# The first two batches of a retention and mixer kernel in another order on every engine, casts moved between engines, and w1 in four tiles

## The chip, the core and the metric

The kernel runs on one core of a Trainium2 chip. The metric is the device time of one execution in microseconds; the time given for a kernel is the median of its runs. The core has five engines that work side by side: TensorE (PE, with its weight loads shown as PEld), VectorE (DVE), ScalarE (ACT), GpSimd (POOL) and SyncE (SP, which here only issues transfers). Each engine takes its instructions strictly in the order in which they are written, and waits where one of them waits.

## The reference, cut

```python
def _attn_ref(q, k, v):                      # q, k, v: [8, 8, 576, 64]
    scores = (1.0 / np.sqrt(64)) * np.matmul(q, k.transpose(0, 1, 3, 2))
    gamma = 1.0 - 2.0 ** (-5.0 - np.arange(8))
    rel = pos[:, None] - pos[None, :]
    Dmat = np.where(rel >= 0, gamma[:, None, None] ** rel[None], 0.0)
    return np.matmul(scores * Dmat[None], v)

def _moe_ref(x, U, V, w_ch1, w_ch2):         # x: [8, 576, 512]
    xt = x.transpose(0, 2, 1)
    h = xt @ U @ V                           # U: [576, 32], V: [32, 576]
    u = x + h.transpose(0, 2, 1)
    ch = np.maximum(u @ w_ch1, 0.0) @ w_ch2  # [512, 2048], [2048, 512]
    return u + ch
```

The first function's heads, laid side by side, are the x of the second. Inputs and output are float32; the kernel computes in bfloat16 with float32 sums.

## The kernel before, in words

The decay of the retention is split into a factor for each query row (`qscale`) and one for each row of V (`vscale`, with the scale of the scores in it). What is left is a causal mask of ones, so a running sum of k times scaled v can be carried from chunk to chunk.

Two batches make a pair: 1,152 rows, nine chunks of 128 rows. Chunk 4, called J, holds the last 64 rows of the first batch (LO) and the first 64 of the second (HI). Later pairs go chunk by chunk through `section`, with their q and k transposed by DMA. The first pair goes by four *units* of 256 rows (0 and 1 in the first batch, 2 and 3 in the second), plus J's halves, and PE transposes it. A unit's q, k and v come as two half tiles each, of four heads (`load_u` on SP's queue). The pool `stage` holds 15 such tiles.

The steps of a unit u are these. `cast_u(u, j, hh, engine)` casts half hh of q (j = 0) or k (j = 1) to bfloat16, and `scale_u` multiplies v by `vscaleU`. `T_u(u, j, engine)` transposes on PE and copies out on the engine named; the copy of q also reorders. `SC_u` makes scores, `mask_u` masks them on DVE (line 674). `ST_u` adds k times v to the sum `acc` in PSUM, and `Sblk` copies its two diagonal blocks to SBUF as state. `RV_u` and `QS_u` add masked scores times v and q times state in the PSUM tile `po`; `XS_u` multiplies by `qscale` on DVE into x (line 712). J has the same steps with `_J`, and `XS_J` is at line 796.

Then comes the mixer of the first batch. `to_xT` transposes x in PSUM with an identity (lines 899 to 905). `MA` multiplies x by U into `a_sb` (line 437). Four matmuls with `V4` (lines 921 to 926) add h in the same PSUM tiles, and four copies on ACT and DVE make `uT` (lines 928 to 934). `make_uo` makes a copy of U shifted by half a chunk for the second batch. `Y1` is the first channel product: for each of 16 blocks f of 128 columns of w1, four matmuls of 512 columns (line 525), then a Relu on ACT (line 530). Y1 tiles rotate over the three PSUM tiles of `ps_big`. `Y2` is the second product (line 559).

w1 is one tile of 2048 columns, cast to bfloat16 on its way. `load_w1(fb)` brings a quarter of it, the columns of blocks 4 fb to 4 fb + 3, and is issued on POOL's queue, as are the pairs of w2 blocks (`load_w2`; `gated_w2` first reads a Y1 result).

The order is written out by hand under `manual_schedule`: `early_consts`, then `startup` (units 0 and 1, J's LO, the first mixer), then `first_stretch` (Y1 blocks of the first batch with units 2 and 3, J's HI and the second mixer between them). `warm(n)` issues n matmuls on the identity whose results nobody reads. From then on `merge` lays the steps of later chunks over the blocks of Y1 and Y2 by shares of their cost. `prep(g)` casts q and k of chunk g, scales v and issues the transpose on SP; its `load` comes earlier. The order list counts the first pair's chunks, so batch 2 begins with chunk NI = 9. For the second batch `merge` starts after six Y1 blocks of its own (`y1_left`); `prep(11)` stands at 0.06 of that stretch.

Of the kernel before, what the change touches and what calls it, by code (L numbers as in the profile page):

```python
# [36 lines left out]
def kernel(  # L37
# [17 lines left out]
    P = 128  # L55
# [59 lines left out]
    w1_sb = consts.tile([P, NCC, dff], BF16, name="w1_sb")  # L115
# [79 lines left out]
    W1B = 512  # L195

    def load_w1(fb):
        nc.gpsimd.dma_start(
            out=w1_sb[:, :, fb * W1B:(fb + 1) * W1B],
            in_=moe_w_ch1[:, fb * W1B:(fb + 1) * W1B].rearrange("(c p) f -> p c f", p=P),  # L200
        )
# [308 lines left out]
    def y1_items(par, by_seg=False):  # L510
# [6 lines left out]
        def Y1(f, seg):  # L517
# [6 lines left out]
            for cc in range(NCC):  # L524
                nc.tensor.matmul(  # L525
                    ps[:, 0:n, :], w1_sb[:, cc, f * P:(f + 1) * P],
                    st["uT", par][:, c0:c0 + n, cc, :],
                    start=(cc == 0), stop=(cc == NCC - 1),
                )
# [67 lines left out]
    def load_u(u, which):  # L597
        b = u // 2
        t0 = 2 * P * (u % 2) + HALF * b
        for j in which:  # L600
            dram = (q, k, v)[j]
            for hh in range(2):
                t = stage.tile([P, H, D], FP32, tag="stage", name="stage_t")
                un[u]["f", j, hh] = t
                nc.sync.dma_start(  # L605
                    out=t.rearrange("p (h j) d -> p h (j d)", j=2),
                    in_=dram[b, 4 * hh:4 * hh + 4, t0:t0 + 2 * P, :].rearrange(
                        "h (p j) d -> p h (j d)", j=2),
                )

# [23 lines left out]
    def T_u(u, j, eng):  # L634
        pst = ps_big.tile([P, 2 * NHP, P], BF16, tag="big", name="pst")
        for jj in range(2):
            for hp in range(NHP):
                nc.tensor.transpose(  # L638
                    pst[:, jj * NHP + hp, :], un[u][j][:, jj, hp * P:(hp + 1) * P], ident)
        t = qkT_pool.tile([P, 2 * NHP, P], BF16, tag="qkT", name="qkT")  # L640
# [7 lines left out]
        if eng is nc.scalar:  # L648
            nc.scalar.activation(out=o, in_=i_, func=AF.Copy)  # L649
        else:  # L650
            eng.tensor_copy(out=o, in_=i_)
# [162 lines left out]
    def pss_tile():  # L814
        return ps_s.tile([P, NHP, P], FP32, tag="pss", name="pss")

    def cast_unit(u):
        for j in (1, 0):
            for hh in range(2):
                cast_u(u, j, hh, nc.gpsimd)  # L820

    def startup():
        load_u(0, (1, 0))
        load_v_rows()
        load_u(1, (1, 0))
        load_u(0, (2,))
        load_u(1, (2,))
        load(0, J, (1, 0, 2), seg=0)
        load_u_rows()
        load(0, J, (1, 0, 2), seg=1)  # L830
        load_u(2, (1, 0, 2))
        load_u(3, (1, 0, 2))
        nc.gpsimd.memset(x_of(0, J)[HI, :], 0.0)

        warm(10)
        cast_unit(0)
        T_u(0, 1, nc.vector)
        warm(5)
        nc.scalar.activation(out=V_b, in_=V_f, func=AF.Copy)
        T_u(0, 0, nc.scalar)  # L840
        make_v()
        warm(3)
        SC_u(0, 0, ps_sc, "psc")
        mask_u(0, 0)
        cast_unit(1)
        T_u(1, 1, nc.scalar)
        SC_u(0, 1, ps_o, "po")
        mask_u(0, 1)
        warm(2)
        T_u(1, 0, nc.scalar)  # L850
        scale_u(0, 0, nc.gpsimd)
        load_w1(0)
        scale_u(1, 0, nc.gpsimd)
        scale_u(1, 1, nc.gpsimd)
        cast_qk(0, J, LO, nc.gpsimd, js=(0,))
        scale_v(0, J, LO, nc.gpsimd)
        load_w1(1)
        cast_qk(0, J, HI, nc.gpsimd)
        scale_v(0, J, HI, nc.gpsimd)
        load_w1(2)  # L860
        scale_u(0, 1, nc.vector)
        warm(6)
        SC_u(1, 0, ps_sc, "psc")
        mask_u(1, 0)
        SC_u(1, 1, ps_o, "po")
        mask_u(1, 1)

        accA = pss_tile()
        accB = ps_big.tile([P, NHP, P], FP32, tag="big", name="pss2")
        ST_u(0, LO, accA, True)  # L870
        Sblk(accA, 0)
        ST_u(0, ALL, accB, True)
        Sblk(accB, 1)
        cast_qk(0, J, LO, nc.scalar, js=(1,))
        po_u(0, ps_sc, "psc")
        warm(2, ps_big, "big")
        RV_u(0, 0)
        RV_u(0, 1)
        QS_u(0, 1, 0)
        XS_u(0)  # L880
        warm(1, ps_big, "big")
        ST_u(1, LO, accB, False)
        Sblk(accB, 2)
        warm(1, ps_big, "big")
        RV_u(1, 0)
        RV_u(1, 1)
        T_J(LO, nc.vector)
        ST_u(1, HI, accB, False)
        Sblk(accB, 3)
        SC_J(LO)  # L890
        mask_J(LO)
        QS_u(1, 0, 1)
        QS_u(1, 1, 2)
        XS_u(1)
        make_ue()

        xT = [ps_big.tile([P, dm], FP32, tag="big", name="xT") for _ in range(3)]

        def to_xT(i, ccs):
            for cc in ccs:  # L900
                nc.tensor.matmul(
                    xT[cc][:, i * P:(i + 1) * P],
                    x_of(0, i)[:, cc * P:(cc + 1) * P], ident,
                    start=(i == 0), stop=True, skip_group_check=True,
                )

        for i in range(2):
            to_xT(i, range(3))
        RV_J(LO)
        QS_J(3)  # L910
        XS_J(LO)
        warm(2, ps_sc, "psc")
        xT.append(ps_sc.tile([P, dm], FP32, tag="psc", name="xT"))
        for i in range(2, J):
            to_xT(i, range(3))
        for i in range(J):
            to_xT(i, (3,))
        MA, _, _, _ = mixer_items(0, 0, split=True)
        MA((ps_o, "po"))
        warm(1)  # L920
        for cc in range(NCC):
            g = slice(cc * R, (cc + 1) * R)
            nc.tensor.matmul(
                xT[cc], st["a", 0][g, :], V4[g, HALF:HALF + 4 * P],
                start=False, stop=True, skip_group_check=True,
            )
        warm(1)
        for cc in range(NCC):
            o = st["uT", 0][:, :, cc, :]
            i_ = xT[cc].rearrange("p (s t) -> p s t", t=P)  # L930
            if cc % 2 == 0:
                nc.scalar.activation(out=o, in_=i_, func=AF.Copy)
            else:
                nc.vector.tensor_copy(out=o, in_=i_)
# [7 lines left out]
    def first_stretch():  # L942

        ys = iter([fn for _, fn in y1_items(0)])

        def y(n):
            for _ in range(n):
                fn = next(ys, None)
                if fn is not None:
                    fn()  # L950

        _, MH0, _, outs0 = mixer_items(0, 0, split=True)
        MA1, MH1, MT1, outs1 = mixer_items(0, 1, split=True)
        y(1)
        make_uo()
        y(3)
        T_J(HI, nc.scalar, ps_s, "pss")
        y(1)
        SC_J(HI)
        mask_J(HI)  # L960
        y(1)
        acc = pss_tile()
        ST_J(HI, acc)
        Sblk(acc, 0)

        def unit(u, slots, last):
            if last:
                load_w1(u)
            for hh in range(2):
                cast_u(u, 1, hh, nc.gpsimd)  # L970
            cast_u(u, 0, 0, nc.gpsimd)
            cast_u(u, 0, 1, nc.gpsimd)
            if last:
                load(*order[NI], (1, 0, 2), gate=True)
                load(*order[NI + 1], (1, 0, 2))
            scale_u(u, 0, nc.gpsimd)
            scale_u(u, 1, nc.gpsimd)
            if not last:
                y(1)
            T_u(u, 1, nc.vector)  # L980
            T_u(u, 0, nc.scalar)
            y(2)
            SC_u(u, 0, ps_sc, "psc")
            mask_u(u, 0)
            y(1)
            ST_u(u, LO, acc, False)
            Sblk(acc, slots[1])
            SC_u(u, 1, ps_sc, "psc")
            mask_u(u, 1)
            if not last:  # L990
                RV_u(u, 0)
                ST_u(u, HI, acc, False)
                Sblk(acc, slots[2])
            else:
                y(1)
                load(*order[NI + 2], (1, 0, 2))
                RV_u(u, 0)
            QS_u(u, 0, slots[0])
            QS_u(u, 1, slots[1])
            RV_u(u, 1)  # L1000
            XS_u(u)
            if last:
                RV_J(HI)
                XS_J(HI)

        unit(2, (0, 1, 2), False)
        unit(3, (2, 3), True)
        load_w2(0)
        load_w2(2)
        load_w2(4)  # L1010
        xT = [None] * NCC

        def to_xT(ccs, chunks):
            for cc in ccs:
                if xT[cc] is None:
# [42 lines left out]
        for f in range(6):  # L1058
            Y1(f, 1)
# [103 lines left out]
```

## Time and profile before

| what | value |
|---|---|
| median of three runs | 319.55 us (318.63 to 320.24) |
| profiled execution | 318.86 us, of which the traced span is 317.1 us |
| PE busy in the span | 306.5 us (97%) |
| DVE, ACT, POOL busy | 165.0, 137.6, 90.8 us |
| granted TensorE clock | 1.00 |
| read from HBM, written to it | 36.85 MB, 9.44 MB |
| first Y1 matmul | 24.36 us from the span's start |
| w1 issues on POOL | 13.30, 19.48, 24.54, 34.94 us |
| w2 issues on POOL, first three | 40.48, 41.24, 41.95 us |

A row of the timeline has the start in microseconds, the duration, the engine, the line, the operation, the tiles it writes and reads, their shapes, and in brackets the idle time of the engine before it and what ended that. The profile is one execution, so its sums are held against its own 318.86 us. Busy time counts `warm` too, and a matmul counts from its issue to its modelled end.

### The profile page before, as it was taken

The numbers are of one execution on the slowest core, as the hardware profiler recorded it, in microseconds if no ns is written. First come the engines' busy times: TensorE is split into PE (matmuls) and PEld (weight loads), VectorE is DVE, ScalarE is ACT, GpSimd is POOL, SyncE is SP. The second block draws the span as 40 slices with busy tenths as digits, with TensorE's granted clock in tenths as the row PEclk, the third lists the DMA queues.
The fourth block names the chain that finished last, engine by engine and source line by source line (L and its number), as shares of the span: only waits on it lengthen the run. The fifth ranks groups of instructions, "written<-read, shape, count | busy, mean of one in ns | idle before, by whom it ended". The sixth has DMA issues, their size and how long they took to land.

```text
span 317.1 us, 9092 instructions
## 1 busy us (share of the span) xinstructions
PE 306.5 (97%) x3903; PEld 168.4 (53%) x3929; DVE 165.0 (52%) x320; ACT 137.6 (43%) x282; POOL 90.8 (29%) x138
## 2 busy tenths in 40 slices
PE   7999899999999999999999999999999999999996
PEld 2564554554544544467744545467654444467544
DVE  5562466535998753892358723992258714200012
ACT  2747657770122474137820474237820453057300
POOL 5765833523241523243221320343211100100000
PEclk9999999999999999999999999999999999999999
DMA  7999999999999999999959899899925104110022
GB/s 211 246 194 258 251 202 205 194 237 209 203 241 190 280 206 199 186 244 190 220 96 215 199 173 193 162 210 245 201 68 138 68 2 83 68 66 1 2 87 79
DMA packets 151320, 53.30 MB, mean 168 GB/s; under 512 B 131984, under 2 KB 148752, under 8 KB 151280
## 3 DMA queue, kind: packets, MB, share of 16 engines
q1 hardware_dynamic: 144512, 40.40, 69.8%
q0 software_dynamic: 6768, 12.32, 16.3%
q8 instruction: 30, 0.49, 0.7%
q14 instruction: 10, 0.08, 0.1%
HBM read 36.85 MB, written 9.44 MB: 146 GB/s over the span
## 4 chain that ended last, share of the span: by engine, by line
PE 83%; DMA 5%; SPq 5%; DVE 3%; issue 2%; ACT 1%; POOL 0%; DVEq 0%; ACTq 0%
PE ps_y L525 37%; PE ps_y L559 36%; DMA w_sb<-in_moe_w_ch_dram 3%; SPq L605 3%; DMA stage_t<-in_v_dram 2%; PE po L377 1%; SPq L233 1%; PE psc L297 1%; PE po L388 1%; PE ph L465 1%; PE ps_y L570 1%; PE inc L314 1%; PE pa L431 1%; DVE ret L327 1%; DVE s_f L349 1%
## 5 line engine op out<-in xcount | busy, mean ns | idle before, releaser
L525 PE MATMUL ps_y<-uT,w_sb 128*128 128x512 bf16 (+3 forms) x768 | 130.5, 326 | 1.0 <-DMA w_sb<-in_moe_w_ch_dram 0.6
L559 PE MATMUL ps_y<-w_sb,y 128*128 128x512 bf16 x534 | 122.6, 379 | 2.7 <-issue 2.1
L530 ACT ACTIVATE y<-ps_y 128x384 bf16<-128x384 f32 (+2 forms) x192 | 89.3, 489 | 50.3 <-PE ps_y L525 49.2
L525 PEld LDWEIGHTS <-w_sb 128*128 128x128 bf16 x768 | 71.0, 98 | 52.6 <-issue 2.1
L559 PEld LDWEIGHTS <-y 128*128 128x128 bf16 x560 | 52.7, 98 | 61.2
L548 DVE TENSOR_TENSOR o_sb<-ps_y,u 128x512 f32<-128x512 f32 (+2 forms) x38 | 25.1, 661 | 55.8 <-PE ps_y L559 53.4
L356 ACT ACTIVATE s_sb<-s_f 128x1024 bf16<-128x1024 f32 (+1 forms) x16 | 14.8, 922 | 82.8 <-DVE s_f L349 76.1
L551 POOL DMA_DIRECT2D out_dram<-o_sb x31 | 17.4, 562 | 113.2 <-DVE o_sb L548 103.6
L258 POOL TENSOR_TENSOR vt<-stage_t,vscale 128x512 bf16<-128x512 f32 (+1 forms) x29 | 30.4, 1047 | 38.1 <-DMA stage_t<-in_v_dram 32.5
L396 DVE TENSOR_TENSOR xt<-po,qscale 128x512 bf16<-128x512 f32 x27 | 17.6, 686 | 44.1 <-PE po L388 44.0
L327 DVE TENSOR_TENSOR ret<-psc,tri 64x512 bf16<-64x512 f32 (+1 forms) x64 | 38.6, 603 | 1.2
L471 DVE TENSOR_TENSOR u<-ph,xt 128x512 bf16<-128x512 f32 (+4 forms) x33 | 22.4, 733 | 13.0 <-PE ph L465 13.0
L249 ACT ACTIVATE qk<-stage_t 128x512 bf16<-128x512 f32 x27 | 16.8, 622 | 11.3 <-DMA stage_t<-in_q_dram 11.3
L247 POOL CAST qk<-stage_t 128x512 bf16<-128x512 f32 x20 | 12.3, 616 | 20.9 <-DMA stage_t<-in_k_dram 9.3
L349 DVE TENSOR_TENSOR s_f<-inc,s_f 128x256 f32<-128x256 f32 x38 | 16.1, 423 | 1.6
L340 DVE COPY vs<-vt 64x256 bf16<-64x256 bf16 x54 | 14.3, 265 | 1.0
L674 DVE TENSOR_TENSOR ret<-psc,triU 128x1024 bf16<-128x1024 f32 x8 | 9.6, 1222 | 9.6 <-PE psc L666 9.6
L192 PE MATMUL pw<-ident 128*128 128x512 bf16 x34 | 10.7, 434 | 1.4 <-POOL ident masks.py:199 1.4
L623 POOL CAST qk<-stage_t 128x512 bf16<-128x512 f32 x16 | 9.7, 616 | 6.3 <-DMA stage_t<-in_k_dram 3.4
L627 POOL TENSOR_TENSOR qk<-stage_t,vscaleU 128x512 bf16<-128x512 f32 x7 | 7.4, 1055 | 4.3 <-DMA stage_t<-in_v_dram 4.1
L377 PEld LDWEIGHTS <-qkT 64*64 64x64 bf16 x384 | 4.7, 108 | 6.4 <-issue 5.9
L649 ACT ACTIVATE qkT<-pst 128x1024 bf16<-128x1024 bf16 x5 | 6.3, 1255 | 2.4 <-PE pst L638 2.4
(115 smaller groups left out, 172.7 us busy)
## 6 DMA issues: line engine op xcount, KB each, us to landing
stage_t<-in_k_dram SPq DMA_DIRECT2D x32, 256.0 KB, 4.9
stage_t<-in_q_dram SPq DMA_DIRECT2D x32, 256.0 KB, 5.4
stage_t<-in_v_dram SPq DMA_DIRECT2D x32, 256.0 KB, 5.8
out_dram<-o_sb POOLq DMA_DIRECT2D x31, 256.0 KB, 4.2
w_sb<-in_moe_w_ch_dram POOLq DMA_DIRECT2D x4, 512.0 KB, 7.8
w_sb<-in_moe_w_ch_dram POOLq DMA_DIRECT2D x8, 256.0 KB, 5.6
stage_t<-in_k_dram SPq DMA_DIRECT2D x8, 128.0 KB, 5.1
stage_t<-in_q_dram SPq DMA_DIRECT2D x8, 128.0 KB, 5.3
```

The lines of the kernel that those rows point to most:

```text
L249: nc.scalar.activation(out=t[rows, 0, :], in_=c["f", 0][rows].rearrange("p h d -> p (h d)"), func=AF.Copy)
L258: (eng or nc.gpsimd).tensor_tensor(out=c["v"][rows], in0=c["f", 2][rows], in1=vscale[rows, i, :, None].to_broadcast([n, H, D]), op=ALU.mult,)
L327: nc.vector.tensor_tensor(out=ret[o, n, 0:m], in0=psc[t, hl, 0:m * D].rearrange("p (b i) -> p b i", i=D), in1=tri[t, None, t].to_broadcast ...
L349: nc.vector.tensor_tensor(out=s_f[:, s, :], in0=src, in1=s_f[:, st["f_end"], :], op=ALU.add)
L356: nc.scalar.activation(out=s_sb[:, 0:n, :], in_=s_f[:, 0:n, :], func=AF.Copy)
L396: nc.vector.tensor_tensor(out=x_of(pr, i).rearrange("p (hp hl d) -> p hl hp d", hl=2, d=D), in0=po[:, :, a * SW:(a + 1) * SW].rearrange("p ...
L471: nc.vector.tensor_tensor(out=st["u", par][:, i0 - base:i0 - base + n, w].rearrange("p s (c d) -> p c s d", c=len(ccs)), in0=t[:, :, 0:n, ...
L525: nc.tensor.matmul(ps[:, 0:n, :], w1_sb[:, cc, f * P:(f + 1) * P], st["uT", par][:, c0:c0 + n, cc, :], start=(cc == 0), stop=(cc == NCC - 1),)
L530: nc.scalar.activation(out=st["y1", par][:, f, c0 * P:(c0 + n) * P], in_=ps[:, 0:n, :].rearrange("p s t -> p (s t)"), func=AF.Relu)
L548: nc.vector.tensor_tensor(out=o_sb[:, 0:n], in0=ps[:, 0:n], in1=st["u", par][:, c, w], op=ALU.add)
L551: (nc.sync if last else nc.gpsimd).dma_start(out=out_flat[r0:r0 + P, w], in_=o_sb[:, 0:n])
L559: nc.tensor.matmul(ps, st["y1", par][:, f, c * P:(c + 1) * P], w2_sb[:, f, :], start=(f == 0), stop=(f == NF - 1),)
```

## The change

w1 becomes four tiles of 512 columns. `startup`, `first_stretch`, `load_u` and `T_u` are replaced by one function, `front`, that lists nearly every step of the first two batches in a new order for each engine; `ld` loads one half tile, and `T_u` is split in `T_pe` (transposes) and `T_cp` (copy). The steps themselves stay. Seven casts of units leave POOL: five go to DVE (k of unit 0 half 1, k half 0 and q half 1 of unit 1, q half 0 of unit 2, k half 1 of unit 3) and two of unit 3 to ACT. The copies of unit 0's and unit 3's transposed q and of J's HI go from ACT to DVE, as does one state copy. The copies of the first uT are dealt anew: cc 1 and 0 on DVE, 3 and 2 on ACT. The transfers of J's k and q stand between those of the units, w1's first three quarters stand behind J's LO on POOL, and the numbers of `warm` matmuls differ.

```diff
-    w1_sb = consts.tile([P, NCC, dff], BF16, name="w1_sb")
+    W1B = 512
+    w1_t = [consts.tile([P, NCC, W1B], BF16, name=f"w1_{n}") for n in range(dff // W1B)]
...
-                    ps[:, 0:n, :], w1_sb[:, cc, f * P:(f + 1) * P],
+                    ps[:, 0:n, :],
+                    w1_t[f * P // W1B][:, cc, f * P % W1B:f * P % W1B + P],
...
-        startup()
-        y1_left = first_stretch()
+        y1_left = front()
```

The function `front`, with several steps on a line; `ys` are the Y1 blocks of the first batch, `Y1(f, seg)` those of the second:

```python
def front():
    ld(0, 1, 1); warm(6); ld(0, 1, 0); ld(0, 0, 1); cast_u(0, 1, 1, DVE); ld(0, 0, 0); ld(1, 1, 0)
    cast_u(1, 1, 0, DVE); load_v_rows(); ld(1, 1, 1); ld(1, 0, 0); ld(1, 0, 1); ld(0, 2, 0)
    load(0, J, (1,), seg=0); ld(0, 2, 1); ld(1, 2, 0); ld(1, 2, 1); load(0, J, (0,), seg=0)
    POOL.memset(x_of(0, J)[HI, :], 0.0); load(0, J, (2,), seg=0); ld(2, 0, 0); po_u(0, ps_sc, "psc")
    warm(12); load_u_rows(); load(0, J, (0,), seg=1); cast_u(0, 1, 0, POOL); ld(2, 1, 0)
    load(0, J, (2,), seg=1); cast_u(0, 0, 1, POOL); ACT.activation(out=V_b, in_=V_f, func=AF.Copy)
    cast_u(0, 0, 0, POOL); load(0, J, (1,), seg=1); ld(2, 1, 1); warm(1); ld(2, 0, 1); ld(2, 2, 0)
    ld(2, 2, 1); ld(3, 1, 0); ld(3, 0, 0); warm(1); ld(3, 1, 1); T_pe(0, 0); T_cp(0, 0, DVE)
    ld(3, 0, 1); cast_u(1, 1, 1, POOL); ld(3, 2, 1); T_pe(0, 1); make_v(); T_cp(0, 1, DVE)
    SC_u(0, 1, ps_o, "po"); ld(3, 2, 0); T_pe(1, 1); T_cp(1, 1, ACT); new_acc(1, ps_big, "big")
    cast_u(1, 0, 0, POOL); scale_u(0, 0, POOL); cast_u(1, 0, 1, DVE); T_pe(1, 0)
    scale_u(1, 0, POOL); mask_u(0, 1); SC_u(0, 0, ps_sc, "psc"); mask_u(0, 0); scale_u(1, 1, POOL)
    warm(7); new_acc(0, ps_s, "pss"); cast_qk(0, J, LO, POOL, js=(0,)); scale_v(0, J, LO, POOL)
    T_cp(1, 0, ACT); SC_u(1, 1, ps_o, "po"); SC_u(1, 0, ps_sc, "psc"); load_w1(0); load_w1(1)
    scale_u(0, 1, DVE); ST_u(0, ALL, acc[1], True); Sblk(acc[1], 1); ST_u(0, LO, acc[0], True)
    RV_u(0, 0); Sblk(acc[0], 0); load_w1(2); cast_qk(0, J, HI, POOL, js=(0,)); mask_u(1, 0)
    mask_u(1, 1); RV_u(0, 1); QS_u(0, 1, 0); XS_u(0); warm(1); warm(1, ps_big, "big"); RV_u(1, 0)
    cast_qk(0, J, LO, ACT, js=(1,)); T_J(LO, DVE); ST_u(1, LO, acc[1], False); Sblk(acc[1], 2)
    warm(2, ps_big, "big"); ST_u(1, HI, acc[1], False); Sblk(acc[1], 3)
    cast_qk(0, J, HI, POOL, js=(1,)); SC_J(LO); mask_J(LO); RV_u(1, 1); QS_u(1, 0, 1); QS_u(1, 1, 2)
    warm(1, ps_big, "big"); warm(3); XS_u(1); to_xT(0, (0, 1, 2), (0,)); RV_J(LO); QS_J(3); XS_J(LO)
    to_xT(0, (0, 1, 2), (1,)); to_xT(0, (0, 1, 2), (2,)); make_ue(); MA0((ps_o, "po"))
    to_xT(0, (0, 1, 2), (3,)); to_xT(0, (3,), range(J)); cast_u(2, 1, 0, POOL); mix_xT(0)
    uT_cp(0, 1, DVE); uT_cp(0, 3, ACT); uT_cp(0, 2, ACT); scale_v(0, J, HI, POOL); make_uo()
    warm(1, ps_sc, "psc"); uT_cp(0, 0, DVE); cast_u(2, 0, 0, DVE); ys[0](); ys[1]()
    T_J(HI, DVE, ps_s, "pss"); cast_u(2, 1, 1, POOL); ys[2](); ys[3](); cast_u(2, 0, 1, POOL)
    ys[4](); scale_u(2, 0, POOL); load(*order[NI], (1, 0, 2), gate=True); ys[5](); ys[6]()
    new_acc(2, ps_s, "pss"); ST_J(HI, acc[2]); Sblk(acc[2], 0); SC_J(HI); mask_J(HI); T_pe(2, 1)
    T_cp(2, 1, DVE); scale_u(2, 1, POOL); T_pe(2, 0); T_cp(2, 0, ACT); ys[7](); ys[8]()
    SC_u(2, 0, ps_o, "po"); mask_u(2, 0); ys[9](); ST_u(2, LO, acc[2], False)
    SC_u(2, 1, ps_sc, "psc"); Sblk(acc[2], 1, (DVE, ACT)); RV_u(2, 0); load_w1(3); QS_u(2, 0, 0)
    cast_u(3, 0, 1, ACT); QS_u(2, 1, 1); ST_u(2, HI, acc[2], False); cast_u(3, 1, 0, ACT)
    Sblk(acc[2], 2); mask_u(2, 1); RV_u(2, 1); cast_u(3, 0, 0, POOL); cast_u(3, 1, 1, DVE)
    T_pe(3, 1); XS_u(2); ys[10](); T_pe(3, 0); T_cp(3, 1, DVE); ys[11](); T_cp(3, 0, DVE)
    SC_u(3, 0, ps_o, "po"); mask_u(3, 0); scale_u(3, 1, POOL); SC_u(3, 1, ps_sc, "psc")
    mask_u(3, 1); scale_u(3, 0, POOL); ST_u(3, LO, acc[2], False); Sblk(acc[2], 3); ys[12]()
    RV_J(HI); XS_J(HI); RV_u(3, 0); QS_u(3, 0, 2); QS_u(3, 1, 3); RV_u(3, 1); XS_u(3); load_w2(2)
    ys[13](); ys[14](); MA1(); to_xT(1, (0, 1), (5, 6)); to_xT(1, (0, 1), (7, 8)); load_w2(4)
    load(*order[NI + 1], (1, 0, 2)); to_xT(1, (2, 3), (5, 6)); to_xT(1, (2, 3), (7, 8)); mix_xT(1)
    uT_cp(1, 0, ACT); uT_cp(1, 1, ACT); ys[15](); prep(NI); load(*order[NI + 3], (1, 0, 2))
    uT_cp(1, 3, DVE); uT_cp(1, 2, DVE); Y1(0, 0); MH1((J,)); load(*order[NI + 2], (1, 0, 2))
    Y1(1, 0); MH0(outs0[0]); MT1((J,)); load_w2(0); Y1(5, 0); Y1(2, 1); Y1(3, 0); gated_w2(8, 3)
    Y1(3, 1); Y1(4, 0); Y1(1, 1); Y1(2, 0); Y1(0, 1); MH1((5, 6, 7, 8)); load_w2(6); Y1(5, 1)
    Y1(4, 1); prep(NI + 1); gated_w2(10, 4); return rest[6:]
```

More of the change, by code (lines that the diff above doesn't have):

```diff
@@ L812, in ST_J @@
                 )
[L814 to L900, printed above, removed]
@@ L913, in startup, with mix_xT @@
[L913 to L920, printed above, removed]
+    def mix_xT(par):
         for cc in range(NCC):
@@ L959, in first_stretch @@
         SC_J(HI)
         mask_J(HI)
[L961 to L1004, printed above, removed]
@@ L1026, in first_stretch @@
[L1026 to L1040 removed]
+        T_pe(2, 1)
@@ new lines, in front @@
+        T_cp(2, 1, DVE)
+        scale_u(2, 1, POOL)
+        T_pe(2, 0)
+        T_cp(2, 0, ACT)
+        ys[7]()
+        ys[8]()
+        SC_u(2, 0, ps_o, "po")
+        mask_u(2, 0)
+        ys[9]()
+        ST_u(2, LO, acc[2], False)
+        SC_u(2, 1, ps_sc, "psc")
+        Sblk(acc[2], 1, (DVE, ACT))
+        RV_u(2, 0)
+        load_w1(3)
+        QS_u(2, 0, 0)
+        cast_u(3, 0, 1, ACT)
+        QS_u(2, 1, 1)
+        ST_u(2, HI, acc[2], False)
+        cast_u(3, 1, 0, ACT)
+        Sblk(acc[2], 2)
@@ L1041, in first_stretch @@
+        XS_J(HI)
+        RV_u(3, 0)
+        QS_u(3, 0, 2)
+        QS_u(3, 1, 3)
+        RV_u(3, 1)
+        XS_u(3)
+        load_w2(2)
+        ys[13]()
+        ys[14]()
+        MA1()
+        to_xT(1, (0, 1), (5, 6))
+        to_xT(1, (0, 1), (7, 8))
+        load_w2(4)
+        load(*order[NI + 1], (1, 0, 2))
+        to_xT(1, (2, 3), (5, 6))
+        to_xT(1, (2, 3), (7, 8))
+        mix_xT(1)
+        uT_cp(1, 0, ACT)
+        uT_cp(1, 1, ACT)
+        ys[15]()
         prep(NI)
-        load_w2(6)
```

317 lines of the change are left out of this document (223 added, 94 removed).

## The prediction

> **What bounds the kernel now.** I read the page first (engines, slices, chain), then the timeline from 0 to 62 us, the waits of PE from 24 to 58 us, and the landings of the w1 transfers. The page:
>
> ```profile
> span 317.1 us, 9092 instructions
> PE 306.5 (97%) x3903; PEld 168.4 (53%) x3929; DVE 165.0 (52%) x320; ACT 137.6 (43%) x282; POOL 90.8 (29%) x138
> ...
> PE   7999899999999999999999999999999999999996
> ...
> DMA  7999999999999999999959899899925104110022
> ```
>
> PE is busy from slice 2 to the end and DMA for the first half. PE's busy share hides that `warm` fills the first 24 us; the useful stream begins at the first Y1 block. From 58 us on no two matmuls start more than 0.35 us further apart than the first of them needs, so the end follows the front one for one: whatever the first two batches lose or win arrives at the end. The timeline, which gives start, duration and engine:
>
> ```profile
> 13.30 0.93 POOL L198 DMA_DIRECT2D w_sb<-in_moe_w_ch_dram  x1
> ...
> 14.63 1.05 POOL L627 TENSOR_TENSOR qk<-stage_t,vscaleU 128x512 bf16<-128x512 f32 x1 [0.40 <-DMA stage_t<-in_v_dram]
> ...
> 16.72 1.23 DVE L712 TENSOR_TENSOR xt<-po,qscale 128x1024 bf16<-128x1024 f32 x1
> ...
> 18.50 1.04 POOL L258 TENSOR_TENSOR vt<-stage_t,vscale 64x512 bf16<-64x512 f32 x1 [0.19 <-DMA stage_t<-in_v_dram]
> ...
> 21.64 0.67 DVE L796 TENSOR_TENSOR xt<-poJ,qscale 64x512 bf16<-64x512 f32 x1
> ...
> 23.71 1.08 ACT L932 ACTIVATE uT<-xT 128x512 bf16<-128x512 f32 x2 [0.48 <-PE xT L923]
> 23.75 1.29 DVE L934 CAST uT<-xT 128x512 bf16<-128x512 f32 x2 [1.43 <-PE xT L923]
> 24.36 1.10 PE L525 MATMUL ps_y<-uT,w_sb 128*128 128x512 bf16 x4 [0.35 <-ACT uT L932]
> ```
>
> Y1 starts at 24.36, released by the copy of uT; the first quarter of w1, issued at 13.30, is there by then. For how long such a quarter takes, the source view of the four w1 transfers:
>
> ```profile
> DMA to landing us min/median/max: 7.5/7.8/9.6
> ```
>
> **The change, part by part.** *w1 in four tiles.* Block 0 already started at 24.36 without the second quarter (issued at 19.48), so the ranges were told apart before; I put this at nothing, bounds nothing either side.
>
> *w1 behind J's rows on POOL.* This is the largest term. Before, the first w1 issue stands after one multiply of V (13.30). In the new order POOL issues it behind `scale_u(0,0)`, `(1,0)`, `(1,1)`, the cast of J's q and `scale_v(0,J,LO)`. J's v is still the 15th stage load, so its rows land between 18.4 (as before) and 17.6 (the 13.1 of unit 0's second v half, at which DVE's multiply starts at 13.16, plus five loads at the 0.9 us by which the POOL casts of early loads are spaced). Unit 1's last v half comes at about 16.2; then 1.06 + 0.60 + 1.04 us of POOL work and three hand-overs give 19.1 for the issue (18.6 to 19.5). Plus 7.8 us: the first quarter lands at 26.9. Bounds: 18.6 + 6.3 = 24.9, where 6.3 lies between the quickest w2 transfer of half the size (5.0) and the quickest of w1 (7.5); and 19.5 + 9.6 = 29.1. Behind the three issues POOL's casts of J's upper half and unit 2 wait 2.4 us (3 x 0.81); their rows are still on the way, so that costs nothing.
>
> *The path of x on DVE.* Three casts and the q copy of unit 0 join DVE ahead of the masks. DVE's constants end at 5.56. The cast of k1 then waits for the fifth load (8.3) and ends at 8.75; the q copy, permuted, comes next: the plain k copy took 0.69 on DVE, ACT's permuted one 1.31 against 1.02 for its plain one, 1024 elements out of PSUM in the masks 1.22. Bounds 0.69 and 1.23, I take 1.15. With the k copy (0.69) the first scores start at 10.75 instead of 10.06; the cast of q1 (0.41) precedes the first mask. Masks of unit 1 then end at 17.6 instead of 16.72, XS of unit 0 at 18.85 instead of 17.95, J's copy and mask 0.75 to 0.9 later. XS of unit 1 ends at 22.8 instead of 21.72, J's RV and QS stand behind four `warm` matmuls (0.9), so XS_J ends at 24.0 instead of 22.3. MA0, its copy (0.28) and the four mixing matmuls (0.39) bring the copies of uT to 25.3, and the copy of cc 0 is DVE's second (2 x 0.645): Y1 could start at 26.7. Bounds: 25.5 (short copy, no hand-over lost) to 27.2. So two paths meet within 0.2 us, and w1 is the later one: start at 26.9 instead of 24.36, **+2.5**; the first block then runs without the 0.1 us hole it has now, **-0.1**. The relief of POOL is worth nothing here, as POOL waits for landings, not the reverse.
>
> A rule of the Trainium skill bears on these casts. The row first: DVE's 128x512 cast took 0.41, but 0.985 when it began at 51.16 inside POOL's multiply (50.82 to 51.85). The page SBUF — State Buffer, section SBUF: two separate sides, says that VectorE in a two-port mode and GpSimd hold a shared port pair in turn, the later one blocked. By it a cast can cost 0.57 more; the rival below takes that up.
>
> *The order after 24 us.* Now PE loses about 2.0 us to waits between 24.36 and 58.6: 0.73 before block 8 (third quarter of w1, at 33.3), 0.39 for a cast of the sums (37.5), 0.22 (40.7), and some 0.6 around the second mixer (48.3 to 50.6).
>
> ```profile
> PEld L525 <- DMA w_sb<-in_moe_w_ch_dram: 1.2, 2, 1.1
> ```
>
> That line is PE's view of w1: one real hold. New: the three first quarters are issued back to back. The three w2 transfers of half the size that are issued so now (40.48 to 41.95) landed 1.5 and 3.2 us apart; at twice that size 3.0 to 6.4, so I put the second and third near 31 and 35. PE reaches blocks 4 and 8 at 31.2 and 36.3. The fourth is behind `scale_u(2,1)` (unit 2's v near 34.5): issue 35.7, landing 43.5, block 12 wanted at 47. The 0.73, 0.39, 0.22 and 0.2 of the mixer (MA1 now precedes its transposes) go: **-1.5** (-2.0 to +1.0, if the second quarter is late by that). What is late next: unit 3's two transposed copies both on DVE (0.69 + 1.15) before its scores, **+0.3** (0 to 1.0); and after the second mixer only one Y1 block covers four copies that take 1.6, where two covered them, **+0.5** (0.2 to 0.7).
>
> The rest (U_O, J's upper half with its copy now on DVE, unit 2's casts, scores and sums, w2's order) costs nothing: Y1 blocks of 0.97 us on PE lie over it, and a block that waited would cost at most its own 0.97.
>
> *Loads of batch 2.* On SP's queue the first transpose (`prep(9)`) now stands ahead of chunk 12, and chunk 12 ahead of 11. The transpose waits for a cast that follows the mixer, near 55.5; chunk 11 then lands near 65 to 69, and its casts on DVE and ACT are due near 65. Queued behind ACT's cast are the Relu copies of Y1, and PE has three PSUM tiles (about 2 us) before it waits for them. Before, chunk 11 was issued at 50.5. **+0.6** (0 to 3.0), near the low end as the cover is there.
>
> Sum: 2.5 - 0.1 - 1.5 + 0.3 + 0.5 + 0.6 = **+2.3 us**. The profiled execution took 318.86 (span 317.1 and 1.8 around it): 321.2. The median of the runs, 319.55, is 0.7 above that execution, so I say **321.9**. A measurement of this kernel tells about 0.5% (1.6 us) from no change.
>
> **The rivals.**
> - *Faster.* Without w1 beside them, J's rows land early: POOL free at 17.9, w1 in at 24.6 (6.7 us), x ready as soon, all 2.0 us of waits gone and nothing new: +0.3 - 2.0 = -1.7, **317.85**. It decides at the first w1 issue: only before 18.0. For: w1's traffic is gone from 15 to 19 us. Against: POOL's own three instructions take 2.7 us after unit 1's v, and x has its own delay. Chance 0.12.
> - *No difference.* First start at 25.5 (low ends of both paths, +1.1), waits repaid with 1.5, 0.5 for the copies: +0.1, about **319.7**. Chance 0.26.
> - *The shared port.* By the rows, two casts on x's path (k1, q1) lengthened by 0.57 each: x at 27.8 instead of 26.7, 0.9 behind w1: **322.8**. Against: POOL is idle from 8.1 to 9.4 and from 11.0 to 12.2, when they run. Chance 0.07.
> - *Worse.* Three w1 transfers on one queue beside SP's hold each other up: the first lands at 29.1 (+2.2 on the forecast) and the second holds block 4, which takes back half of the -1.5: **324.9**. For: the slowest of the four took 9.6 while SP's loads were deep in the queue, as they will be. Against: the w2 triple's first took 5.1. Chance 0.13.
> - *Nothing done*, the order given on paper only: excluded, since the present trace shows POOL's and SP's instructions in the written order.
>
> **How the numbers follow.** The forecast itself has 0.42. Slower: 0.42 + 0.07 + 0.13 = 0.62; within 0.5%: 0.26; faster 0.12. The likeliest case alone spans 320.5 to 324. The range reaches down to the faster rival's edge and up past the worse one: 318.2 to 325.8, leaving out about 0.1 on each side.
>
> **What would show it.** Right: the first w1 issue on POOL near 19, the first L525 matmul near 27 with DMA of w1 as its releaser, masks of unit 1 ending near 17.6, XS_J near 24; no w1 wait at block 8; chunk 11's loads issued after 57. Wrong: a first Y1 block before 25, a w1 issue before 18, or PE waiting on ACT for more than 2 us between 62 and 72.

## The result, and the profile after

The changed kernel takes 328.26 us (median of 6 runs, 326.1 to 332.36), the kernel before 319.19 (6 runs beside it): a ratio of 1.0275, 95% interval 1.0232 to 1.0319. Ratios, here and below, leave out runs more than 1.5% above the fastest run of the same kernel, so they can differ from the ratio of two medians. The changed kernel is slower by about 9 us. The forecast was slower by 2.3 us, 321.9 with a range up to 325.8: the direction was right, the size far too small. The profiled execution of the changed kernel took 328.79 us, its span is 326.4.

First the page of the changed kernel: span, engines, the slices of PE, the granted clock and DMA.

```profile
span 326.4 us, 9128 instructions
PE 313.5 (96%) x3931; PEld 169.7 (52%) x3931; DVE 170.9 (52%) x329; ACT 135.6 (42%) x280; POOL 87.5 (27%) x131
...
PE   8887999959999999999999999999999999999996
...
PEclk9997999998999999999999999999999999999999
DMA  7999995999999999999996979799967102310012
```

A slice is 8.2 us. PE's row has a 5 in the ninth slice (65.3 to 73.4), where it had 9s. The clock row, all nines before, has a 7 in the fourth slice and an 8 in the tenth: right behind the two places where PE waits. DMA's seventh slice, 49 to 57 us, reads 5. The waits of PE from 24 to 82 us (total, times, longest):

```profile
PE ps_y L524 <- ACT y L530: 3.6, 1, 3.6
PE ps_y L524 <- DMA w<-in_moe_w_ch_dram: 1.1, 1, 1.1
```

Before, this view had a hold by w1 at block 8 and nothing near 70 us. Now there is one wait for w1 at the start, and one of 3.6 us for the Relu copies. The timeline shows both in their order:

```profile
18.20 1.04 POOL L257 TENSOR_TENSOR vt<-stage_t,vscale 64x512 bf16<-64x512 f32 x1
...
19.18 2.44 POOL L197 DMA_DIRECT2D w<-in_moe_w_ch_dram  x3
...
23.62 0.68 DVE L782 TENSOR_TENSOR xt<-poJ,qscale 64x512 bf16<-64x512 f32 x1 [0.54 <-PE poJ L775]
...
27.61 3.35 PE L524 MATMUL ps_y<-uT,w 128*128 128x512 bf16 x8 [1.08 <-DMA w<-in_moe_w_ch_dram]
...
45.12 3.49 SPq L232 DMA_DIRECT2D stage_t<-in_v_dram  x1
...
55.33 1.34 SPq L265 DMA_TRANSPOSE qkT<-qk  x1
...
69.96 0.63 ACT L248 ACTIVATE qk<-stage_t 128x512 bf16<-128x512 f32 x1 [3.84 <-DMA stage_t<-in_q_dram]
70.50 1.40 ACT L530 ACTIVATE y<-ps_y 128x512 bf16<-128x512 f32 x4
71.12 6.40 PE L524 MATMUL ps_y<-uT,w 128*128 128x128 bf16 x36 [3.63 <-ACT y L530]
```

Read from the bottom. PE stood 3.63 us for a Relu copy; that copy was queued behind ACT's cast of chunk 11's q; that cast waited 3.84 us for its rows; the rows came late, because SP's queue issued nothing between 48.6 (45.12 + 3.49) and the transpose at 55.33, and chunk 11 stood behind that transpose and behind chunk 12. In the kernel before, chunk 11 was issued at 50.5, ahead of that transpose.

How much later each landmark of the useful stream comes, in the two profiled executions:

| landmark | before | after | later by |
|---|---|---|---|
| first Y1 matmul | 24.36 | 27.61 | 3.25 |
| Y1 block 4 | 28.39 | 33.14 | 4.75 |
| first step behind the second mixer (`MH`) | 51.67 | 55.12 | 3.45 |
| first Y2 matmul | 70.17 | 78.93 | 8.76 |
| last matmul | 313.90 | 323.22 | 9.32 |

So 3.45 us are lost up to the second mixer, 5.3 us between it and Y2 and 0.6 later.

### The profile page after: what moved, and what is told of

Its sections match the earlier page's. It is cut to its first block, busy times and chain, and to the rows that moved or that the text cites. A ratio compares the mean times of both kernels' runs of the same rounds, so it can differ in the third digit from the quotient of the medians.

```text
span 326.4 us, 9128 instructions
## 1 busy us (share of the span) xinstructions
PE 313.5 (96%) x3931; PEld 169.7 (52%) x3931; DVE 170.9 (52%) x329; ACT 135.6 (42%) x280; POOL 87.5 (27%) x131
## 4 chain that ended last, share of the span: by engine, by line
PE 80%; DMA 10%; SPq 3%; DVE 3%; ACT 1%; issue 1%; POOL 1%; DVEq 0%; ACTq 0%
PE ps_y L524 37%; PE ps_y L559 33%; DMA stage_t<-in_q_dram 3%; DMA w<-in_moe_w_ch_dram 3%; DMA uT<-u 2%; SPq L848 2%; DMA stage_t<-in_v_dram 2%; PE po L376 1%; PE psc L296 1%; PE ps_y L570 1%; PE po L387 1%; PE ph L464 1%; PE pa L430 1%; PE inc L313 1%; SPq L232 1%
## 5 line engine op out<-in xcount | busy, mean ns | idle before, releaser
L524 PE MATMUL ps_y<-uT,w 128*128 128x512 bf16 (+3 forms) x768 | 132.8, 331 | 4.9 <-ACT y L530 3.6
L559 PE MATMUL ps_y<-w_sb,y 128*128 128x512 bf16 x560 | 126.2, 379 | 0.0
L530 ACT ACTIVATE y<-ps_y 128x512 bf16<-128x512 f32 (+1 forms) x192 | 89.1, 489 | 55.2 <-PE ps_y L524 54.1
L524 PEld LDWEIGHTS <-w 128*128 128x128 bf16 x768 | 72.2, 99 | 59.4 <-issue 8.1
L395 DVE TENSOR_TENSOR xt<-po,qscale 128x512 bf16<-128x512 f32 x27 | 17.6, 686 | 43.8 <-PE po L387 43.7
L246 POOL CAST qk<-stage_t 128x512 bf16<-128x512 f32 x20 | 12.5, 623 | 21.3 <-DMA stage_t<-in_k_dram 15.9
L339 DVE COPY vs<-vt 64x256 bf16<-64x256 bf16 x54 | 16.3, 302 | 1.0
L193 PE MATMUL pw<-ident 128*128 128x512 bf16 x36 | 12.1, 473 | 2.1 <-POOL ident masks.py:199 1.4
L720 DVE COPY qkT<-pst 128x1024 bf16<-128x1024 bf16 (+1 forms) x7 | 5.4, 783 | 6.1 <-PE pst L735 4.4
L609 POOL CAST qk<-stage_t 128x512 bf16<-128x512 f32 x9 | 6.1, 674 | 6.9 <-DMA stage_t<-in_q_dram 3.5
```

Source lines behind the costliest of these rows:

```text
L339: nc.vector.tensor_copy(out=c["vs"][o], in_=v[HALVES[1 - hl], hl])
L395: nc.vector.tensor_tensor(out=x_of(pr, i).rearrange("p (hp hl d) -> p hl hp d", hl=2, d=D), in0=po[:, :, a * SW:(a + 1) * SW].rearrange("p ...
L524: nc.tensor.matmul(ps[:, 0:n, :], w1_t[f * P // W1B][:, cc, f * P % W1B:f * P % W1B + P], st["uT", par][:, c0:c0 + n, cc, :], start=(cc == ...
L530: nc.scalar.activation(out=st["y1", par][:, f, c0 * P:(c0 + n) * P], in_=ps[:, 0:n, :].rearrange("p s t -> p (s t)"), func=AF.Relu)
L559: nc.tensor.matmul(ps, st["y1", par][:, f, c * P:(c + 1) * P], w2_sb[:, f, :], start=(f == 0), stop=(f == NF - 1),)
```

## The experiments

"The changed kernel" is the one after. Every ratio is against the kernel before on the same chip, with its 95% interval, and a loss in us is the ratio's, on 319 us.

**Chunk 11's load ahead of chunk 12's, in the changed kernel.**

```diff
         prep(NI)
-        load(*order[NI + 3], (1, 0, 2))
+        load(*order[NI + 2], (1, 0, 2))
...
         MH1((J,))
-        load(*order[NI + 2], (1, 0, 2))
+        load(*order[NI + 3], (1, 0, 2))
```

> The changed kernel with the loads of chunks 11 and 12 exchanged on SP, so that 11 is issued first after the transpose of chunk 9. Theory A (order of loads): chunk 11's q lands near 62 to 64 instead of 69.9, ACT's cast of it no longer holds the Relu copies, PE's 4.0 us hole at 67.1 and the half-clock matmuls after it (8 x 0.21 = 1.7 us) go: 5 us less, about 323. Theory B (late start: everything arrives late because w1 arrives late, the hole is only where it shows): at most 1 us less, about 327 to 328.

Measured: 326.87 us, ratio 1.0181 (1.0101 to 1.0261), in place of 1.0275: 3.0 us less, though the intervals overlap. The hole at 67 is gone and Y2 starts 2.9 us sooner, at 76.00; but the last matmul comes only 1.3 sooner, at 321.93. The waits of PE from 22 to 155 us:

```profile
PE ps_y L524 <- DMA w<-in_moe_w_ch_dram: 2.5, 1, 2.5
PE psc L296 <- DMA qkT<-qk: 1.6, 2, 0.9
PE ps_y L524 <- ACT y L530: 1.4, 1, 1.4
```

The first line is the start's wait for w1, 1.1 in the changed kernel: this edit doesn't touch it, but this execution began Y1 0.9 later, at 28.55. The other two are new. Later chunks' transposed q and k (`qkT`) are late now, and the Relu copies wait at 75.78 behind ACT's cast of the next chunk's q, which waited 2.09 us for its rows. So the exchange hands part of the wait on; the order of 11 and 12 is only part of it.

**The same wait, moved by the user of the load.** `prep(11)` from 0.06 to 0.19 of its stretch.

```diff
-                (0.06, 0.20, 0.32, 0.47, 0.60, 0.73, 0.90)),
+                (0.19, 0.20, 0.32, 0.47, 0.60, 0.73, 0.90)),
```

> The changed kernel with the casts of chunk 11 placed later in the stretch of the second batch (share 0.19 instead of 0.06, some 8 us into it instead of 2.5), loads unchanged. Theory A: ACT and DVE reach the casts near 71, when q (69.9) is there, so the hole goes although the load is as late as before: 4 to 5 us less, 323 to 324. Theory B: no more than 1 us less. If the transpose of chunk 11 then comes too late for its scores, the hole moves to the first scores of chunk 11 and under 2 us are won.

Measured: 327.51, ratio 1.0268 (1.0218 to 1.0319): no gain that can be told from the changed kernel's own ratio. In its profile the hole shrinks to 0.4 us, Y2 starts at 73.76, 5.2 us sooner, and the last matmul comes only 2.0 sooner, at 321.19. PE's waits for transposed chunks grow instead (22 to 155 us again):

```profile
PE psc L296 <- DMA qkT<-qk: 2.2, 3, 1.0
...
PE ps_y L524 <- ACT y L530: 0.4, 1, 0.4
```

The windows view shows what the transfers moved meanwhile. Its columns are the stretch in us, its length, five engines' busy time, the granted clock, the DMA share and GB/s. The kernel before:

```profile
48.60:55.30 6.70, 6.65 (x77) 3.10 (x77) 4.18 (x7) 5.01 (x11) 2.79 (x3) 1.00 0.95 202
55.30:65.00 9.70, 9.70 (x93) 5.71 (x91) 5.00 (x8) 7.47 (x20) 4.66 (x9) 1.00 1.27 198
```

The changed kernel:

```profile
48.60:55.30 6.70, 6.70 (x98) 3.55 (x90) 3.93 (x6) 3.50 (x9) 0.00 (x0) 1.00 0.62 121
55.30:65.00 9.70, 9.70 (x108) 5.49 (x101) 5.80 (x7) 7.29 (x19) 4.24 (x8) 1.00 0.85 166
```

It moved 81 GB/s less for 6.7 us and 32 less for 9.7: 0.85 MB, which at the 209 GB/s of its next ten microseconds is 4.1 us of transfers. This does not show that the missing transfers are the loss. The exchange, the later `prep` and the warm start below are written like the changed kernel up to the transpose, apart from five `warm` matmuls, and show 161, 176 and 85 GB/s in the first stretch: it scatters that much by itself. The kernel before with the late load alone, further below, misses nothing there and loses all the same.

**A warm start of Y1.** Six `warm` matmuls instead of one ahead of the first Y1.

```diff
-        warm(1, ps_sc, "psc")
+        warm(6, ps_sc, "psc")
```

> The changed kernel with 6 instead of 1 warm matmuls ahead of the first Y1 block, in the time in which PE waits for w1 (26.15 to 27.6). If the half rate of the first Y1 matmuls (427 ns from 28.2 to 30.3) comes from PE's idle time just before, they run at 216 ns: 1.3 us less, about 327. If it comes from the earlier, sparse stretch (15 to 25 us), or if the loads are what counts (theory A, with the start hidden by the later hole), no change: 328.

Measured: 328.44, ratio 1.0299 (1.0255 to 1.0344): no change. Yet the edit did what it was to do: from the first Y1 (28.27) to block 4 it took 3.90 us instead of 5.53, all at full rate. What the start won, the later place took: PE's wait for the Relu copy behind chunk 11's cast is 1.9 us longer, since PE comes there 1.0 sooner and the cast of chunk 11's q starts 0.95 later, at 70.91. Y2 starts at 79.91.

```profile
PE ps_y L524 <- ACT y L530: 5.5, 1, 5.5
```

So in the changed kernel it is chunk 11's load that sets the end up to there, and a start that is better by 1 us is worth nothing until the load is mended.

**Chunk 11's load late, in the kernel before.** This is the same cause alone.

```diff
-                load(*order[NI + 2], (1, 0, 2))
                 RV_u(u, 0)
...
         load(*order[NI + 3], (1, 0, 2))
+        load(*order[NI + 2], (1, 0, 2))
         prep(NI + 1)
```

> The kernel before with only the order of three loads changed as in the change: chunk 11's load moved from ahead of chunk 9's transpose to behind chunk 12's load. Theory A: q of chunk 11 lands near 64 to 66, ACT's cast of it is due near 62.7, a hole of 1 to 3 us on PE and perhaps half-clock matmuls behind it: 320.5 to 324. Theory B (only the late start counts): no change, 319.2.

Measured: 322.82, ratio 1.0113 (1.007 to 1.0156): 3.6 us slower. The wait of the changed kernel is there in a kernel that has none of its other edits, with the same line of 36 matmuls behind it:

```profile
65.37 6.40 PE L525 MATMUL ps_y<-uT,w_sb 128*128 128x128 bf16 x36 [2.21 <-ACT y L530]
```

Its transfers in the two stretches of above:

```profile
48.60:55.30 6.70, 6.70 (x58) 3.05 (x55) 4.76 (x8) 5.39 (x11) 2.16 (x5) 1.00 1.22 206
55.30:65.00 9.70, 7.85 (x80) 4.61 (x78) 4.06 (x7) 5.62 (x16) 2.45 (x5) 1.00 1.14 205
```

They move as much as in the kernel before (202 and 198), and SP stands for 2.0 us ahead of the transpose instead of 6.7. What is late is chunk 11, and that is enough for a loss.

**Chunk 11's load back in its place, in the changed kernel.**

```diff
         load(*order[NI + 1], (1, 0, 2))
+        load(*order[NI + 2], (1, 0, 2))
...
         MH1((J,))
-        load(*order[NI + 2], (1, 0, 2))
```

> The changed kernel with the load of chunk 11 issued ahead of chunk 9's transpose, right after chunk 10's, as it stood before; chunk 12's stays where the change has it. Theory C (the stream of loads on SP stands still while the transpose waits, and the loss moves on with the stream when one hole is closed): q of chunk 11 lands near 56, no hole at 67, the stream of later loads is back at the lag of the late start (about 3 us), and nothing is given back later: 323 us or a little less. Theory B (the late start alone): 327 to 328.

Measured: 323.23 (320.82 to 325.31), ratio 1.0121 (1.0029 to 1.0212). One load, moved ahead of one transpose, gives 5 of the 9 us back. No hole is left at 67; Y2 starts at 72.13 and the last matmul at 315.88. The stretch that moved 121 GB/s moves 211:

```profile
48.60:55.30 6.70, 6.70 (x84) 3.13 (x81) 3.41 (x6) 4.19 (x9) 0.62 (x1) 1.00 1.10 211
```

**w1 issued early as well.** The kernel just shown, with the first quarter of w1 right behind `scale_u(0, 0)` as in the kernel before.

```diff
         scale_u(0, 0, POOL)
+        load_w1(0)
...
-        load_w1(0)
         load_w1(1)
```

> The kernel of e5 with the first quarter of w1 issued after the first multiply of V, as before (near 13.7 instead of 19.2). If the late first quarter costs what the prediction says plus the half-clock matmuls, the first Y1 block starts near 26.7 when x is there and runs at full rate: 2 to 3 us less than e5, about 320.5. If w1's traffic then holds back J's rows and x by as much, no gain over e5: 323.

Measured: 323.15, ratio 1.0122 (1.0055 to 1.0188): no gain is seen, though with these intervals one of some 2 us isn't excluded. The rows of the timeline:

```profile
14.58 0.93 POOL L197 DMA_DIRECT2D w<-in_moe_w_ch_dram  x1
19.86 1.04 POOL L257 TENSOR_TENSOR vt<-stage_t,vscale 64x512 bf16<-64x512 f32 x1
...
25.49 0.68 DVE L782 TENSOR_TENSOR xt<-poJ,qscale 64x512 bf16<-64x512 f32 x1 [0.54 <-PE poJ L775]
28.66 1.89 PE L524 MATMUL ps_y<-uT,w 128*128 128x512 bf16 x8 [0.27 <-DVE uT L720]
```

The wait for w1 is gone; the first Y1 waits for the copy of uT. J's v is multiplied at 19.86 instead of 18.49, and `XS_J` ends at 26.17 instead of 24.62. That w1's 512 KB push x back would explain it, but it isn't shown: in this execution the cast of unit 1's q (12.43 instead of 11.35) and the first multiply of v (13.58 instead of 12.82) were 0.8 to 1.1 us late already, ahead of the issue of w1 at 14.58. What the run does show is that a start with w1 in time is held by x.

**w1 late, in the kernel before.** Its first three quarters behind J's v, nothing else.

```diff
         scale_u(0, 0, nc.gpsimd)
-        load_w1(0)
...
         scale_v(0, J, LO, nc.gpsimd)
+        load_w1(0)
         load_w1(1)
+        load_w1(2)
...
-        load_w1(2)
```

> The kernel before with one thing changed: the first three quarters of w1 issued back to back behind the multiply of J's first v rows, as in the change. With loads in their old order no later hole hides it: the first Y1 block starts near 27 instead of 24.36, part of the 2 us of waits is repaid, and two to eight Y1 matmuls may run at half rate: 321 to 323.5. If the later loads hide it, 319.

Measured: 323.87, ratio 1.0135 (1.0056 to 1.0214), 4.3 us slower. The issue at 19.04 and the first Y1 at 28.29, 3.9 later than before. The wait, and the stretch behind it in the windows view, where the clock is half:

```profile
28.29 1.89 PE L525 MATMUL ps_y<-uT,w_sb 128*128 128x512 bf16 x4 [4.47 <-DMA w_sb<-in_moe_w_ch_dram]
...
28.30:33.00 4.70, 4.70 (x12) 1.75 (x13) 0.00 (x0) 1.65 (x4) 1.23 (x2) 0.50 1.20 220
```

Ten Y1 matmuls stand 427 ns apart instead of 216: 2.1 us on top of the wait.

**The third quarter of w1 early, in the kernel before,** to see whether its hold at block 8 was worth anything.

```diff
         load_w1(1)
+        load_w1(2)
         cast_qk(0, J, HI, nc.gpsimd)
         scale_v(0, J, HI, nc.gpsimd)
-        load_w1(2)
```

> The kernel before with the third quarter of w1 issued right behind the second (20.3 instead of 24.5), ahead of the casts of J's upper half. The hold of 0.73 us at block 8 goes if it lands near 31: 0.3 to 0.7 us less, 318.3. If the loads of unit 2, which it displaces, arrive later than they are wanted, 319 to 321.

Measured: 319.56, ratio 1.002 (0.9978 to 1.0061): no difference. The hold at block 8 is gone. PE waits twice for the casts of unit 2's q instead (0.8 and 0.6 us, their rows come later), and 0.73 us for w1's fourth quarter at 43.87.

**The path of x alone, in the kernel before.** The three casts of units 0 and 1 on DVE, and DVE's copy of unit 0's transposed q.

```diff
-                cast_u(u, j, hh, nc.gpsimd)
+                cast_u(u, j, hh, nc.vector if (u, j, hh) in ((0, 1, 1), (1, 1, 0), (1, 0, 1)) else nc.gpsimd)
...
-        T_u(0, 0, nc.scalar)
+        T_u(0, 0, nc.vector)
```

> The kernel before, with only the path of x made as in the new one: the casts of k half 1 of unit 0 and of k half 0 and q half 1 of unit 1 are on DVE, and DVE copies unit 0's transposed q out of PSUM. w1 and all loads stay. Theory (the x path alone is a term of about 1 to 2 us, and in the changed kernel w1's late landing lies over it): masks of unit 1 end 0.5 to 1.5 us later than before, the first Y1 starts at 25 to 26 instead of 24.36, and nothing gives it back, so 320 to 321. Rival (POOL relieved is worth as much as DVE's longer path): no difference, 319.3 within 0.5.

Measured: 320.24, ratio 1.0049 (1.0013 to 1.0084), about 1.6 us slower. The masks of unit 1 end at 19.35 and the first Y1 starts at 26.94, 2.6 late, by the copy of uT. The DVE rows show the order at work:

```profile
10.17 1.23 DVE L674 TENSOR_TENSOR ret<-psc,triU 128x1024 bf16<-128x1024 f32 x1 [0.52 <-PE psc L666]
11.31 0.75 DVE L623 CAST qk<-stage_t 128x512 bf16<-128x512 f32 x2
```

Two casts of unit 1 are written behind unit 0's first mask here and wait for it, and unit 1's transposes with them. In the changed kernel both stand ahead of the masks, and its masks end at 18.14. So this experiment is a harsher case of the step, not its exact price in the changed kernel.

**Both single causes together, in the kernel before:** the late load of chunk 11 and the late w1, the two diffs above in one kernel.

> The kernel before with both single edits of the earlier runs: chunk 11's load behind chunk 9's transpose and chunk 12's load (alone +3.6 in its batch), and w1's first three quarters behind J's v (alone +4.6). If the two losses add up: 319.3 + 8 = 327.5, as slow as the changed kernel, with a hole of 4 us near 24 and another of 2 to 3 near 63. Rival (one hides the other, since a later start leaves the load more time): the hole near 63 shrinks by what the start loses, and the time is 323.5 to 325.

Measured: 327.14, ratio 1.0263 (1.0213 to 1.0313), beside 1.0275 (1.0232 to 1.0319) of the changed kernel. That is 8.4 us where 3.6 and 4.3 make 7.9: the two losses add up, and two edits of where transfers stand make the kernel before as slow as the whole change. PE's waits from 22 to 82 us:

```profile
PE ps_y L525 <- DMA w_sb<-in_moe_w_ch_dram: 5.2, 1, 5.2
PE ps_y L525 <- ACT y L530: 1.7, 1, 1.7
```

The rival was half right in the trace: the second wait is 0.5 shorter than the 2.21 it was alone. The time followed the sum all the same. The waits are not divided as in the changed kernel, though: 5.2 and 1.7 here, 1.1 and 3.6 there. The equal time alone doesn't show that the parts are equal.

**The old start with the new rest.** The start of the kernel before up to the copies of uT, then the changed kernel's order, with chunk 11's load in its old place.

```diff
     def front():
-        ld(0, 1, 1)
...
-        uT_cp(0, 0, DVE)
+        startup()
+        cast_u(2, 1, 0, POOL)
+        make_uo()
         cast_u(2, 0, 0, DVE)
         ys[0]()
...
         load(*order[NI + 1], (1, 0, 2))
+        load(*order[NI + 2], (1, 0, 2))
```

> The first 24 us as before (the loads, casts, w1 issues and the first mixer of the kernel before) and everything from the second Y1 stretch on as in the new kernel, with chunk 11's load back behind chunk 10's. Theory (the start and chunk 11's load are all that the change loses, and its order after the start repays about 1.5 us of waits): first Y1 at 24.4, last matmul at 312 to 313, 317.5 to 318.5, faster than before by 0.3 to 0.5%. Rival (the order after the start is worth nothing, or loses by its later loads of batch 2): 319 to 321.

Measured: 320.54 (317.74 to 326.09, 12 runs), ratio 1.0012 (0.9975 to 1.005): level with the kernel before. Its profiled execution, the fastest of its runs, had the last matmul at 312.81, inside the theory's 312 to 313. But its first Y1 stood at 23.39, 1.0 sooner than in the kernel before, and its last matmul 1.1 sooner: the lead comes from the start, and the order behind it repaid next to nothing where 1.5 us were expected. The median bears out no gain either. No version here beats the kernel before.

## Why the prediction was right or wrong

**The start: right in its steps, a little short.** The first w1 issue was forecast at 19.1 and came at 19.18; its landing at 26.9 and came at 27.56; the masks of unit 1 at 17.6 and ended at 18.14; XS of unit 1 at 22.8 (23.09), XS_J at 24.0 (24.30); the copies of uT were to make Y1 possible at 26.7 and ended at 26.75. So the two paths met as said, w1 the later one, and the term of +2.5 measured 3.25. Of the three w1 transfers that were issued back to back, at 19.18, 20.10 and 20.85, the landings were 27.56, 31.25 and 34.90: near 31 and 35, as written, and no block waited for the second or third. The rival in which they hold each other up to 29.1 did not come. That the two paths stand this close fits the run in which w1 was issued early: the first Y1 then waited for uT, and no gain was seen. w1 alone costs 4.3 us in the kernel before, where the copies of uT begin at 23.5 and PE then waits 4.5 us for w1.

**The first step that failed: the rate of PE behind a wait.** The sum had "the first block then runs without the 0.1 us hole it has now, -0.1". It counted waits, and took matmuls after a wait at 216 ns. In the changed kernel the first four blocks took 5.53 us instead of 4.03. The granted clock by windows:

```profile
27.60:33.00 5.40, 5.39 (x24) 2.19 (x25) 0.43 (x1) 1.72 (x3) 0.62 (x1) 0.68 1.20 220
33.00:55.00 22.00, 21.43 (x342) 12.34 (x340) 13.51 (x16) 14.01 (x28) 8.83 (x13) 1.00 1.04 213
...
66.50:71.20 4.70, 1.07 (x9) 0.43 (x7) 1.30 (x4) 1.24 (x4) 0.00 (x0) 1.00 1.30 222
71.20:75.50 4.30, 4.30 (x22) 2.23 (x22) 0.00 (x0) 2.23 (x7) 2.93 (x4) 0.62 0.89 176
```

The clock column is 0.68 and 0.62 in the stretches that follow the two waits: 6 Y1 matmuls of 427 ns behind the first (6 x 0.21 = 1.3 us) and 8 behind the second (1.7 us). The forecast had no term for this. The first 1.3 us were hidden in this kernel, as the warm start showed; the second lie in the stretch between the mixer and Y2, behind the wait for chunk 11.

The Trainium skill, page TensorE: Matmul & The Clock Gate, section Part 1: The HAM clock gate, puts the half rate behind an idle window of about 3.4 us. The section Why this matters for your kernels of the same page of the Trainium skill asks for no idle gap above some 3 us between bursts of matmuls. The wait of 3.6 us agrees. The first one doesn't: 1.46 us from the start of the last `warm` matmul (26.15) to the first Y1, in a stretch from 24.0 to 27.6 in which PE was busy for 1.98 us, was enough in this execution. The same gap at the same place was 1.53 us with the later `prep` and 1.40 with chunk 11's load moved, and both ran on at full rate. The measurement decides: a gap of this size may or may not do it, and its length alone doesn't tell.

**The terms that were right.** The repaid waits (-1.5), unit 3's copies (+0.3) and the copies behind the second mixer (+0.5) were to bring -0.7 together; from block 4 (4.75 late) to the first step behind the mixer (3.45 late) the stream won 1.3 back. No wait for w1 is left at block 8. w1 in four tiles changed nothing that can be seen; no run has it alone. The shared port cost nothing on the two casts of its rival: those of unit 1's k and q took 0.43 (at 7.97) and 0.41 (at 11.65), with POOL idle beside them, as the forecast argued. Where the engines did meet, either could pay. In the changed kernel DVE's multiply of v began at 14.74 and took 0.68, and POOL's began at 14.76 and took 1.57 instead of 1.06; in the warm start POOL's began first, at 14.67, and took 1.06, and DVE's began at 14.69 and took 1.59. The rule of the Trainium skill that the forecast weighed (SBUF — State Buffer, SBUF: two separate sides) has the later instruction blocked, and these two pairs agree. One row looks otherwise: a POOL cast that began at 4.73 took 1.16 instead of 0.62, beside a DVE cast from 5.07 to 5.42 that took 0.35. It ended at 5.88 or 5.89 in five other kernels with this start too, whether it had begun at 4.68 or at 4.81; what held it isn't settled.

**The mis-sized term: chunk 11.** "+0.6 (0 to 3.0), near the low end as the cover is there" is the step that sank the forecast: moving the load back was worth 4.9 us. Everything ahead of the size was right: the transpose at 55.5 (55.33), chunk 11's landing between 65 and 69 (its q at 69.9), its cast on ACT with the Relu copies queued behind it, and PE with some 2 us in three PSUM tiles. The text even named the sign, "PE waiting on ACT for more than 2 us between 62 and 72". What it did not do is put these together: a q at 69.9 and a cast due at 66.1 is 3.84 us of ACT's idle time, and the PSUM tiles carried PE only to its last matmul at 67.11, 1.0 us. With the cast and the first Relu copy still to come after the landing, 3.63 us reach PE. With the 1.7 us at half rate that is 5.3, as much as the landmarks lose between the mixer and Y2. The forecast also priced only the first load behind the transpose, where the exchange and the later `prep` show that closing the one hole makes later chunks' waits appear. Whether the 0.85 MB that did not move between 48.6 and 65 us are a cause or a companion stays open. By the ratios the exchange gave back 3.0 us, the later `prep` 0.2, the moved load 4.9; by the last matmul of the profiled executions 1.3, 2.0 and 7.3.

**Shown and open.** Shown, each alone on the kernel before: the late load costs 3.6 us, the late w1 4.3, both together 8.4. Shown on the changed kernel: moving the one load back is worth 4.9 us. With it the kernel is still 3.9 us above the one before by the ratio of 1.0121, and 2.0 by the profiled execution, which was the fastest of its four runs. That this rest is the start, w1 and x together, is argued from the first Y1 at 27.87 and from the old start with the new rest, which differs from that kernel in the start and came out level (0.9975 to 1.005 beside 1.0029 to 1.0212); how it divides between w1 and x was not separated. Whether the new order after the start wins anything by itself stays open, within half a per cent.

## What to carry to other kernels

When a step with a wait of its own is put ahead of loads on an in-order queue, work out the landing and the due time of each load behind it, and not of the first alone: when the first user's wait was closed here, others appeared. When several engines' covers are in series (a load, a cast, the copies queued behind the cast, the PSUM tiles), work out the landing minus the due time and subtract each cover once, instead of setting the term near the low end because there is cover. And allow for matmuls at half rate behind a wait of PE: 6, 8 and 10 of them, 1.3 to 2.1 us, stood behind three of the waits here, and none behind some others.

## What was not expected of the hardware

The half rate sets in late: PE resumed at 27.61 and the first 427 ns interval began at 28.20; behind the wait that ended at 71.12 it began at 72.57. Nor does every wait bring it: with the late load alone in the kernel before, a wait of 2.21 us that ended at 65.37 was followed by a granted clock of 0.50; with late w1 and late load, one of 1.69 us that ended at 71.28 by a clock of 1.00. The two stretches, in this order:

```profile
66.50:69.50 3.00, 3.00 (x15) 1.62 (x14) 0.00 (x0) 1.48 (x4) 1.81 (x3) 0.50 0.89 166
```

```profile
70.00:76.00 6.00, 4.72 (x43) 2.72 (x45) 0.35 (x1) 4.73 (x13) 2.92 (x4) 1.00 1.07 178
```

A 512 KB quarter of w1 that was issued alone at 13.30 was no bar to a start at 24.36; three in a row took 8.4, 11.2 and 14.0 us from issue to landing, so they came 3.7 us apart. And the issue and landing of the first, with this start all but unchanged, scattered: in five kernels that share it (the changed one, and those with the chunks exchanged, the later `prep`, the warm start and the moved load) the first Y1 stood at 27.61, 28.55, 29.53, 28.27 and 27.87. A start forecast to 0.2 us is finer than these transfers allow.
